# One queue for the bulk loads, and block 1's convolution inputs turned by TensorE

## The chip, the cores and the metric

The kernel runs on one NeuronCore of a Trainium2 chip. A core has a matrix engine (TensorE, called PE in the profile; its weight loads are the row PEld), a vector engine (VectorE, DVE), a scalar engine (ScalarE, ACT), a general engine (GpSimd, POOL) and a sync engine (SyncE, SP), which here only issues transfers. All read and write one on-chip memory, SBUF, of 128 partitions; PE writes to a second one, PSUM. Transfers (DMAs) are issued by SP, ACT or POOL and carried by 16 DMA engines. SP's transfers run on one queue (q1 in the profile), ACT's on q10, POOL's on q0. The metric is the device time of one execution in microseconds (us); lower is better.

## The reference

The inputs are bfloat16: q, k, v of 2048 x 640, filters `ssm_k` of 640 x 2048, four taps per channel (`shift_k`), a vector `ssm_D`, and the three weight matrices of a gated feed-forward layer (640 x 1728 twice, 1728 x 640).

```
k_shift[s] = sum over t of k[s + t - 3] * shift_k[:, 3 - t]     # a causal convolution with 4 taps
kv         = k_shift * v
y          = irfft(rfft(kv, padded) * rfft(ssm_k, padded))[:S]   # a causal convolution as long as the sequence
y          = y + kv * ssm_D
h          = q + layernorm(q) * y
h2         = h + (silu(LN(h) @ w_gate) * (LN(h) @ w_up)) @ w_down
```

## The kernel before

The sequence is cut into four blocks of 512 rows (`block_j`, j = 0 to 3), the 640 channels into two halves of 320 (`c`). A block's rows are laid out four to a partition, b = 0 to 3.

The long convolution is done by a transform written as matmuls. `fwd` (L585) does the first stage: a matmul per b with a constant table, a copy from PSUM to SBUF, and four transfers ("shuffles", named `sh`) that regroup partitions. It is called for the filter (K) and for kv (X) of each block and half. `spec` (L609) is the second stage, 16 or 32 small 32 x 32 matmuls per step; `swap` (`sw`) exchanges real and imaginary rows by two transfers; `product` multiplies spectra on DVE; `inv2` goes back, and four transfers named `rs` regroup again. `conv_bp` ends the convolution, multiplies by the layer norm of q and adds q. All these shuffles are SBUF-to-SBUF transfers issued by SP. For block j the products use this block's and earlier blocks' spectra, so block j needs the filter's and kv's block j.

What feeds this stage, k, v and the filters, is prepared in two ways:

- Block 0 (`kv_first`, L550): k is loaded as plain rows (`KN0`), turned by PE (`kr`, into `KTR`), and the four taps are matmuls with diagonal matrices (`DIAG`, built by `diag`) that add up in PSUM (`kvp`, 24 matmuls for each b); DVE multiplies by v (`kvv`). The filter is loaded by ACT's queue (`kraw00`, `kraw01`) and turned by PE (`k_natural`, L521).
- Blocks 1 to 3 (`load_kv`, L484, and `kv_block`, L734): k is loaded with its three preceding rows (`kin`), and v (`vin`), both on POOL's queue; DVE multiplies by the taps and adds (4 multiplies, 3 adds, 1 product with v for each half, on 128 x 1280 elements). For blocks 2 and 3 the adds are accumulating transfers on POOL (`KACC`). The filter (`load_kraw`, L498, where `KDMA` is true) is loaded by a transposing transfer (`kraw`), stored to DRAM (`kst`) and loaded again (`kld`) to get four rows to a partition, all on SP.

After the convolution of a block, `ln_bp` normalizes h, PE turns it (`tr`) and a copy puts it into `HNT` (`te`). `ffn_pair` computes the gate and up products of two groups of 128 columns (`gu`), `ffn_b` the down-projection (`dn`), the final add (`fa`) and the store (`st`). The weights are loaded once, by `load_weights` (L894), in 18 pieces on POOL's queue; each piece waits for the piece before the last, and the first two for a product of block 0's kv. q of block 0 (`x0`) is loaded by SP, of the later blocks by POOL (`load_x`).

Nothing is ordered at run time. Every operation is given a number when the program is built, and `_PLAN` (L1058 on) lists all operations in one order with the engine that does each one; this gives each engine its own fixed list. An entry such as `46,4,0,594` is operation 46, on engine 4 (0 PE, 1 ACT, 2 DVE, 3 POOL, 4 SP), then two planned numbers, of which only the order and the choice of buffers and semaphores follow, and for some a letter for the PSUM pool. An engine goes through its list in order and waits, where a buffer or an input needs it, on semaphores (`Prog.emit`, L130). So an operation that waits holds up everything behind it on its engine, and on SP it holds up the issue of all later transfers.

Helpers carry most of the lines that the profile shows: L425 issues every plain transfer, L434 is nearly every matmul, L416/L417 and L419/L420 are copies out of PSUM, L637 is every two-operand DVE operation, L504 a transposing transfer, L535 and L561 are the transposes of block 0's filter and k.

Of the kernel before, what the change touches and what calls it, by code (L numbers as in the profile page):

```python
# [279 lines left out]
def bass_sequential_preLN__ssm_conv_h3__swiglu_ffn__prompt_kernel(  # L280
# [6 lines left out]
    R = 4  # L287
# [6 lines left out]
    KDMA = [False, True, True, True]  # L294
# [13 lines left out]
    with ExitStack() as es:  # L308
# [71 lines left out]
        WROW = P.tile("wrow", None, P.poolbases["TMP"][0])  # L380
        P.pool("KRAW", slots(1, 4 * CW), True)
        P.pool("KT", slots(1, 4 * CW), True)
        P.pool("TB", slots(2, 8 * CW), True)
        P.pool("UK", slots(10, 2 * CW), True)
# [3 lines left out]
        P.pool("SK", slots(4, 8 * CW), True)  # L388
        P.pool("E", slots(4, 4 * CW), True)
# [33 lines left out]
        def dma(subs, kb, reads, writes, prio, eng="sp", after=(), name="", kind="load"):  # L423
            kw = dict(accum_op=ALU.add) if kind == "acc" else {}
            fns = [(lambda g, d=d, s=s: g.dma_start(d(), s(), **kw)) for d, s in subs]  # L425
            return P.op({eng: (0.9 if eng == "pool" else 0.5) * len(subs)}, fns, reads, writes, prio, after=after, dma=(kb, kind), name=name)
# [23 lines left out]
        dma([(lambda: V(WROW, 0, 4 * D, 0, 1), lambda: dram(A_shift_k, 0, [[4 * D, 1], [1, 4 * D]]))], 5, [], [(WROW, 0)], 40, name="taps")  # L450
# [17 lines left out]
        def taps_natural(prio):  # L468
            for k in range(4):
# [13 lines left out]

        def load_kv(j, c, prio):  # L484
# [4 lines left out]
            def rows(p0, p1):  # L489
# [4 lines left out]
            dma(subs, 560, [], [(kt, 0)], prio, name=f"kin{j}{c}", eng="pool", after=turned[:1])  # L494
            dma([(lambda: V2(vt, 0, CW, 4, CW), lambda: dram(V2d, B * j * D + c * CW, [[R * D, 128], [D, 4], [1, CW]]))],
                328, [], [(vt, b) for b in range(4)], prio + 1, name=f"vin{j}{c}", eng="pool", after=turned[:1])

        def load_kraw(j, c, prio):  # L498
            if KDMA[j]:
# [6 lines left out]
                    [], [(t, 0)], prio, after=turned[:1], dma=(328, "turn"), name=f"kraw{j}{c}")  # L506
# [9 lines left out]
        def load_x(j, prio):  # L516
            t = xts[j] = P.tile(f"x{j}", "XH")
            dma([(lambda: V(t, 0, 4 * D), lambda: dram(X2, B * j * D, [[R * D, 128], [1, R * D]]))], 655, [],
                [(t, (b, c)) for b in range(4) for c in range(2)], prio, name=f"x{j}", eng="pool" if j else "sp", after=[kv_last[0, 0]] if j == 1 else ())
# [28 lines left out]
        turned = []  # L548

        def kv_first(prio):  # L550
            dma([(lambda: V(KN0, 0, 4 * D), lambda: dram(K2, 0, [[R * D, 128], [1, R * D]]))], 655, [], [(KN0, 0)], 10, name="kn0")
            for c in range(2):
                dma([(lambda c=c: V2(VIN0, c * 4 * CW, CW, 4, CW), lambda c=c: dram(V2d, c * CW, [[R * D, 128], [D, 4], [1, CW]]))],
                    328, [], [(VIN0, (c, b)) for b in range(4)], 12, name="vin0")
            for h in range(2):
                def turn(h):
                    pt = P.tile("pkr", "pC")
                    fns = []
                    for k in range(2):
                        for d in range(5):  # L560
                            fns.append(lambda t, k=k, d=d: t.transpose(B16(pt, k, d * 128, 128), V(KN0, (2 * h + k) * D + d * 128, 128), V(IDN, 0, 128)))  # L561
                    cells = [(KTR, 2 * h + k) for k in range(2)]
                    turned.append(pe(fns, 128, 10, [(KN0, 0), (IDN, 0)], [(pt, 0)], prio, reserve=cells, name=f"kr{h}"))
                    src = lambda: psb[:, 2 * pt.base:2 * pt.base + 2048].rearrange("p (k d e) -> p k d e", k=2, e=128)[:, :, 0:5, :]
                    evac(lambda: V3(KTR, h * 260 + 2, 130, 2, 520, 5, 128), src, 1280, [(pt, 0)], cells, prio, fast=True, name=f"kre{h}")
                turn(h)
            for b in (3, 0, 1, 2):
                def out(b):
                    pt = P.tile("pkv", "pC")
                    fns = []  # L570
                    for c, d, o, n in ((0, 0, 0, 128), (0, 1, 128, 128), (0, 2, 256, 64), (1, 2, 0, 64), (1, 3, 64, 128), (1, 4, 192, 128)):
                        for t_ in range(4):
# [3 lines left out]
                                          lambda d=d, bb=bb, sh=sh: V(KTR, d * 520 + bb * 130 + sh, 128),  # L576
                                          lambda w0=w0, n=n: V(DIAG, w0, n), t_ == 0, t_ == 3))
                    pe(fns, 128, 24, [(KTR, i) for i in range(4)] + [(KTR, "z")] + [(DIAG, d) for d in range(5)], [(pt, 0)], prio,
                       reserve=[(VIN0, (c, b)) for c in range(2)], name=f"kvp{b}")
                    vv = lambda: V2(VIN0, b * CW, 4 * CW, 2, CW)  # L580
                    kv_last[0, b] = vec(dve1(640), tt(vv, lambda: B32x2(pt, CW), vv, ALU.mult),
# [602 lines left out]
```

## Time and profile before

| what | us |
|---|---|
| time, median of 3 runs | 344.53 (343.39 to 345.29) |
| profiled execution: time | 347.39 |
| profiled execution: span, first to last instruction | 345.5 |
| PE busy | 276.2 (80% of the span) |
| DVE busy | 204.2 (59%) |
| ACT busy | 174.2 (50%) |
| POOL busy | 47.7 (14%) |
| chain that ended last: PE 48%, DMA 26%, ACT 9%, DVE 9%, issue 4%, SP's queue 3% | |

The profile is of one execution. Its page gives for each engine the busy time, and, in 40 equal slices of the span, tenths of busy time (9 is 90% or more); `PEclk` is the clock that was granted to PE, in tenths of the full one; `DMA` the mean busy share of the 16 DMA engines and `GB/s` what they moved. The chain of waits is followed back from the last instruction, at each step to what released it. Other answers of the trace used below are the instructions in order of time, and the busy time of each engine in stretches that are named by their start and end in us. There the columns are the length, then PE, PEld, DVE, ACT, POOL (busy us and number of instructions), the granted clock, the DMA share and GB/s. Shares over 1 come from packets that overlap.

### The profile page before, as it was taken

Reading aid. Unit: us, or ns where it says so; the run is one execution under the profiler, and the core shown is the slowest. Engines: PE = TensorE matmul, PEld = TensorE weight load, DVE = VectorE, ACT = ScalarE, POOL = GpSimd, SP = SyncE. Lnnn points to the kernel's source line nnn. Section 1 sums busy time; section 2 is a strip of 40 time slices with the busy share of each in tenths; the row PEclk is TensorE's granted clock in tenths of the full one; section 3 lists DMA queues with packets and bytes.
Section 4 is the critical chain, followed back from the end, with each engine's and each line's share of the span. In section 5 each row is a group of like instructions: output and inputs, shape, how many; then the busy total and the mean of one; then the engine's idle time right before and its main releaser. Section 6 shows DMA issues by size and latency. Waiting matters only on the chain.

```text
span 345.5 us, 8043 instructions
## 1 busy us (share of the span) xinstructions
PE 276.2 (80%) x3366; PEld 144.6 (42%) x3392; DVE 204.2 (59%) x356; ACT 174.2 (50%) x260; POOL 47.7 (14%) x64
## 2 busy tenths in 40 slices
PE   0986535424869989999799999366989999999996
PEld 0741111111424435754244556123444457544474
DVE  3586757655736848783278767738678682212502
ACT  1657967424853854527777625269736332132100
POOL 0231214302220013221121000102100020000000
PEclk9995555655899999999999999856799999999999
DMA  7869999999889749448464324662351200100001
GB/s 222 251 201 348 303 392 308 331 119 346 220 230 256 185 96 284 138 117 238 134 191 110 135 84 174 181 222 77 115 193 58 98 2 21 57 0 2 0 19 59
DMA packets 41352, 56.27 MB, mean 163 GB/s; under 512 B 12562, under 2 KB 31795, under 8 KB 41316
## 3 DMA queue, kind: packets, MB, share of 16 engines
q1 hardware_dynamic: 34788, 37.11, 33.4%
q0 software_dynamic: 5024, 17.94, 20.4%
q10 hardware_dynamic: 1504, 0.69, 0.7%
q8 instruction: 27, 0.44, 0.5%
q14 instruction: 9, 0.07, 0.1%
HBM read 19.03 MB, written 4.59 MB: 68 GB/s over the span
## 4 chain that ended last, share of the span: by engine, by line
PE 48%; DMA 26%; ACT 9%; DVE 9%; issue 4%; SPq 3%; ACTq 0%; DVEq 0%; POOLq 0%
PE ps L434 46%; DMA sb<-sb 21%; ACT sb L416 7%; DVE sb L637 7%; SPq L425 3%; DMA sb<-in_A_ssm_k_dram 2%; DMA out_dram<-sb 1%; ACT sb L419 1%; DMA sb<-in_A_q_dram 1%; ACT sb L721 1%; DVE stt L683 1%; DVE sb L417 1%; PE ps L887 1%; PE ps L535 1%; ACT sb L928 0%
## 5 line engine op out<-in xcount | busy, mean ns | idle before, releaser
L434 PE MATMUL ps<-sb 128*128 128x512 bf16 (+4 forms) x1066 | 192.4, 334 | 5.8 <-ACT sb L928 2.6
L637 DVE TENSOR_TENSOR sb<-sb 128x1280 bf16<-128x1280 bf16 (+3 forms) x152 | 110.1, 762 | 50.8 <-DMA sb<-sb 21.8
L434 PEld LDWEIGHTS ps<-sb 128*128 128x128 bf16 x1092 | 98.9, 98 | 85.7 <-issue 6.3
L434 PE MATMUL ps<-sb,tab 32*32 32x320 bf16 (+1 forms) x2176 | 81.8, 348 | 51.4 <-DMA sb<-sb 25.4
L416 ACT ACTIVATE sb<-ps 128x640 bf16<-128x640 f32 (+1 forms) x129 | 88.8, 747 | 62.8 <-PE ps L434 47.0
L434 PEld LDWEIGHTS ps<-sb,tab 32*32 32x32 f16 (+1 forms) x2176 | 35.6, 92 | 99.8 <-issue 39.9
L637 DVE TENSOR_TENSOR sb<-ps,sb 128x640 bf16<-128x640 f32 (+3 forms) x50 | 42.1, 846 | 58.7 <-PE ps L434 57.2
L928 ACT ACTIVATE sb<-ps 128x1024 bf16<-128x1024 f32 (+2 forms) x32 | 29.3, 916 | 42.3 <-PE ps L434 42.0
L942 ACT ACTIVATE sb<-ps 128x1024 bf16<-128x1024 f32 x18 | 18.5, 1025 | 21.8 <-PE ps L434 15.5
L419 ACT ACTIVATE sb<-ps 128x640 bf16<-128x640 f32 x31 | 20.3, 706 | 17.5 <-PE ps L434 17.4
L708 POOL TENSOR_TENSOR stt<-stt 128x2 f32<-128x2 f32 (+1 forms) x12 | 12.4, 1034 | 72.4 <-DVE stt L706 72.4
L695 DVE TENSOR_SCALAR sb<-sb,stt 128x320 bf16<-128x320 bf16 (+1 forms) x48 | 16.8, 391 | 5.3 <-PE ps L887 3.1
L425 POOL DMA_DIRECT2D sb<-sb x12 | 10.9, 909 | 51.6 <-DVE sb L637 45.9
L683 DVE BATCH_NORM_STATS2 stt<-sb 128x6 f32<-128x320 bf16 x40 | 17.6, 478 | 0.1
L417 DVE CAST sb<-ps 128x640 bf16<-128x640 f32 x12 | 9.8, 822 | 10.3 <-PE ps L434 10.3
L535 PE MATMUL ps<-sb 128*128 128x128 bf16 (+1 forms) x24 | 3.7, 254 | 8.6 <-DMA sb<-in_A_ssm_k_dram 8.6
L721 ACT ACTIVATE sb<-sb 128x640 bf16<-128x640 bf16 x12 | 8.8, 733 | 3.2 <-DMA sb<-in_A_q_dram 3.1
L729 ACT ACTIVATE sb<-sb,stt 128x640 bf16<-128x640 bf16 x12 | 10.0, 836 | 0.2
L425 POOL DMA_DIRECT2D sb<-in_A_v_dram x6 | 4.7, 788 | 35.6 <-PE ps L434 35.6
L425 POOL DMA_DIRECT2D sb<-in_A_k_dram x6 | 6.0, 1000 | 25.1 <-DVE sb L637 13.9
L809 DVE SCALAR_TENSOR_TENSOR sb<-ps,sb 128x640 bf16<-128x640 f32 x8 | 6.4, 817 | 2.9 <-PE ps L434 2.9
L887 PE MATMUL ps<-sb 128*128 128x128 bf16 x80 | 7.2, 250 | 0.2
(27 smaller groups left out, 46.6 us busy)
## 6 DMA issues: line engine op xcount, KB each, us to landing
sb<-sb SPq DMA_DIRECT2D x160, 160.0 KB, 3.9
sb<-sb POOLq DMA_DIRECT2D x12, 320.0 KB, 4.5
sb<-in_A_k_dram POOLq DMA_DIRECT2D x6, 560.0 KB, 6.2
out_dram<-sb SPq DMA_DIRECT2D x16, 160.0 KB, 2.2
sb<-in_B_w_gate_dram POOLq DMA_DIRECT2D x5, 416.0 KB, 6.2
sb<-in_B_w_up_dram POOLq DMA_DIRECT2D x5, 416.0 KB, 6.6
sb<-in_A_v_dram POOLq DMA_DIRECT2D x6, 320.0 KB, 4.9
k_nat<-sb SPq DMA_DIRECT2D x6, 320.0 KB, 5.9
```

Source lines behind the costliest of these rows:

```text
L416: fns = {"act": lambda a: a.activation(out=dst(), in_=src(), func=ACTF.Copy), "dve": lambda v: v.tensor_copy(out=dst(), in_=src())}
L417: "dve": lambda v: v.tensor_copy(out=dst(), in_=src())}
L419: fns = {"act": lambda a: a.activation(out=dst(), in_=src(), func=ACTF.Copy, scale=scale), "dve": lambda v: v.tensor_scalar(out=dst(), in0 ...
L425: fns = [(lambda g, d=d, s=s: g.dma_start(d(), s(), **kw)) for d, s in subs]
L434: return lambda t: t.matmul(o(), l(), r(), start=st, stop=sp)
L637: return lambda v: v.tensor_tensor(out=o(), in0=a(), in1=b_(), op=op)
L683: vec(dve1(CW, False), lambda v: v.bn_stats(st6(l, j, b, c), V(xt, b * D + c * CW, CW)), [(xt, (b, c))], [(ST, ("s", j, b, c))], prio, nam ...
L695: vec(dve4(n), lambda v: v.tensor_scalar(out=dst(), in0=src(), scalar1=m, scalar2=rs(l, j, b), op0=op, op1=ALU.mult), reads + [(ST, cell), ...
L708: P.op({"pool": 1.05}, lambda g: g.tensor_tensor(out=y, in0=va, in1=stt[:, 420:420 + hi - lo], op=ALU.pow), c1 + [(ST, "half")], c3, prio, ...
L721: P.op({"act": act_c(D) + 0.05}, lambda a, b=b, jk=jk: a.activation(out=V(jk, 0, D), in_=V(xt, b * D, D), func=ACTF.Copy, accum_out=tmv(l, ...
L928: P.op({"act": act_c(n)}, lambda a: a.activation(out=dst(), in_=src(), func=ACTF.Silu), rd, wr, -1000, name=f"si{j}{i}")
L942: P.op({"act": act_c(1024)}, lambda a: a.activation(out=V(ub, 0, 1024), in_=B32x2(u, 512), func=ACTF.Copy), [(u, 0), (u, 1)], [(ub, 0)], - ...
```

## The change

Bulk loads move to SP's queue. `load_kv`, `load_x` and `load_weights` lose their `eng="pool"`, and with it the waits that spread the loads in time (`turned`, `kv_last`, the chain of weight pieces). Two waits are new: block 2's first k and v loads wait for the last readers (`users`) of buffers that now hold block 1's data.

Block 1 is prepared as block 0 is. `kv_first` becomes `kv_pe(j)` and is called for j = 0 and j = 1: k as rows, 20 transposes on PE, 96 diagonal matmuls, 4 products on DVE, and for j = 1 a small copy (`hal`) that takes the last rows of block 0's turned k as the halo. v is loaded in one transfer per block. The filter of block 1 is loaded for both halves in one transfer (`krf1`) and turned by 20 transposes on PE (`k_one`). Block 1's transposing loads, stores and second loads, its `kin` and `vin` and its `kv_block` are gone. `fwd` gets a `step` for the new layout.

The taps' row buffer moves, the cost of an SP issue in the planner goes from 0.5 to 0.62, and `_PLAN` is new (1129 operations for 1136). On SP's list 227 issues stand for 202 (195 operations for 170; 32 of them, the swaps, issue two), on POOL's 12 for 45. The new SP list begins: tab0, drow, kn0, x0, krf1, vf0, x1, vf1, wg1, wu0, wg3, taps, wu2, wu4, tab1, kn1, the four shuffles shK00, wu1, wg2, three of shX00, wg4, the fourth, gul, swW000, wg0, three of shK01, swW001, the fourth, wu3, rs00h1, swW010, rs00h0, the four shX01, rs00h2, rs00h3, two of shK10, a piece of wd, swW011, another of wd, two of shK10, swW100, the four rs01, and then the four shX10. The transposing loads of blocks 2 and 3 stand so: kraw20 after rs10h0 and before shX11G0, kraw21 after kld20 and before rs11h3, kraw30 after kst21 and before shK20G0, kraw31 between shuffles of shX21. Before, kraw20 stood after kld11 and before swW011, and kraw21 between the last rs01 and shK11G0. On PE's list, 6 steps stand between block 1's last down-projection and block 2's first gate group, where 21 stood.

```diff
-    KDMA = [False, True, True, True]
+    KDMA = [False, False, True, True]
...
+        KN = [KN0, P.tile("kn1", None)]
+        KTRS = [KTR, P.tile("ktr1", None, P.poolbases["KIN"][0] + 8 * CW)]
+        VF = [VIN0, P.tile("vf1", None, P.poolbases["KIN"][0])]
+        KRF = P.tile("krf", None)
+        KT1 = P.tile("kt1", None, P.poolbases["KRAW"][0])
+        WROW = KN0
...
+        def users(*ts):
+            return [o for o in P.ops if any(t in ts for t, _ in o.reads)]
...
-            dma(subs, 560, [], [(kt, 0)], prio, name=f"kin{j}{c}", eng="pool", after=turned[:1])
+            late = users(KTRS[1], VF[1]) if (j, c) == (2, 0) else ()
+            dma(subs, 560, [], [(kt, 0)], prio, name=f"kin{j}{c}", after=late)
...
-                [(t, (b, c)) for b in range(4) for c in range(2)], prio, name=f"x{j}", eng="pool" if j else "sp", after=[kv_last[0, 0]] if j == 1 else ())
+                [(t, (b, c)) for b in range(4) for c in range(2)], prio, name=f"x{j}")
...
-        def kv_first(prio):
-            dma([(lambda: V(KN0, 0, 4 * D), lambda: dram(K2, 0, [[R * D, 128], [1, R * D]]))], 655, [], [(KN0, 0)], 10, name="kn0")
...
+        def kv_pe(j, prio):
+            kn, ktr, vf = KN[j], KTRS[j], VF[j]
+            dma([(lambda: V(kn, 0, 4 * D), lambda: dram(K2, B * j * D, [[R * D, 128], [1, R * D]]))], 655, [], [(kn, 0)], 10 if j == 0 else 30, name=f"kn{j}")
+            dma([(lambda: V(vf, 0, 4 * D), lambda: dram(V2d, B * j * D, [[R * D, 128], [1, R * D]]))],
+                655, [], [(vf, b) for b in range(4)], 12 if j == 0 else 31, name=f"vf{j}")
+            if j:
+                halo.append(vec(0.2, lambda v: v.tensor_copy(out=V3(ktr, 1, 520, 5, 130, 4, 1), in_=V3(KTRS[0], 129, 520, 5, 130, 4, 1)),
+                                [(KTRS[0], i) for i in range(4)], [(ktr, "z")], prio, name="hal"))
...
+        def k_one(prio):
+
+            dma([(lambda: V2(KRF, 0, B, 5, B), lambda: dram(A_ssm_k, B, [[S, 128], [128 * S, 5], [1, B]]))], 655, [], [(KRF, 0)], 29, name="krf1")
+            old = users(kts[0, 0])
+            for h in range(2):
+                def turn(h):
+                    pt = P.tile("pKT", "pC")
+                    fns = []
+                    for k in range(2):
+                        for d in range(5):
+                            def f(t, k=k, d=d):
+                                a = sb[:, KRF.base + d * B + 2 * h + k:KRF.base + d * B + 2 * h + k + 1]
+                                src = bass.AP(a.tensor, a.offset, [list(a.ap[0]), [R, 128]])
+                                return t.transpose(B16(pt, k, d * 128, 128), src, V(IDN, 0, 128))
+                            fns.append(f)
...
+            if j == 1:
+                UKt[j, c] = fwd(f"K{j}{c}", KT1, lambda b: b, c * CW, "UK", pb + 99, D)
...
+            if j > 1:
                 kv_block(j, c, pb + 100)
...
             def piece(subs, kb, cells, nm):
-                chain.append(dma(subs, kb, [], cells, 35, eng="pool", after=(chain[-2:-1] or [kv_last[0, 0]]) + (front if nm[:2] == "wd" else []), name=nm))
+                dma(subs, kb, [], cells, 35, after=front if nm[:2] == "wd" else [], name=nm)
...
-            for c in range(2):
+            for c in range(2 if j != 1 else 0):
...
             if j == 0:
+                k_one(300)
+                kv_pe(1, 301)
                 taps_natural(500)
```

## The prediction

> **What bounds the kernel now.** I read the page's slices first. TensorE (PE) is busy 80% of the span, but not evenly: from about 26 us to 105 us its digits fall to 2-6, the granted clock is 0.5 for most of that stretch, and the DMA row stands at 9. After that PE is nearly full, with one dip near 60% of the span, where the clock falls again.
>
> ```profile
> PE   0986535424869989999799999366989999999996
> ...
> PEclk9995555655899999999999999856799999999999
> DMA  7869999999889749448464324662351200100001
> ```
>
> Then the chain of waits in order of time, for the first 100 us. Its long pieces are SBUF-to-SBUF transfers (columns: start, length, what): the regrouping of each conv step, called shuffles here.
>
> ```profile
> 20.37 2.22 DMA sb<-sb
> ...
> 26.78 5.19 DMA sb<-sb
> ...
> 37.85 8.06 DMA sb<-sb
> ...
> 53.80 5.64 DMA sb<-sb
> ...
> 61.12 7.59 DMA sb<-sb
> ...
> 70.54 10.35 DMA sb<-sb
> ...
> 82.86 4.62 DMA sb<-sb
> ...
> 98.34 3.52 DMA sb<-sb
> ```
>
> These are all 160 KB or pairs of it. In a quieter queue the same step takes 3.52 us at 98.34 and 3.89 us at 125.66, so I call 3.7 us its uncrowded price. What crowds it is seen in the timeline and in busy time by stretch (PE, weight loads, DVE, ACT, POOL, clock, DMA share, GB/s):
>
> ```profile
> 64.15 6.28 SPq L504 DMA_TRANSPOSE sb<-in_A_ssm_k_dram  x1
> ```
>
> ```profile
> 2.40:12.40 10.00, 3.78 (x29) 2.79 (x30) 4.65 (x9) 1.75 (x2) 0.19 (x1) 1.00 0.97 293
> 72.00:74.00 2.00, 1.04 (x5) 0.60 (x6) 0.28 (x1) 0.00 (x0) 0.00 (x0) 0.50 1.37 53
> 80.00:84.00 4.00, 2.33 (x52) 0.69 (x52) 0.33 (x1) 1.78 (x4) 1.87 (x3) 0.50 1.04 390
> 213.50:229.00 15.50, 7.47 (x170) 3.54 (x169) 9.83 (x13) 6.75 (x11) 1.35 (x2) 0.75 0.71 220
> 229.00:246.00 17.00, 13.41 (x223) 6.98 (x224) 12.80 (x29) 14.75 (x29) 2.05 (x2) 0.62 0.33 121
> ```
>
> Behind the transposing load of block 2 (kraw21) the DMA engines are fully busy and move 53 GB/s; a few us later they move 390. While PE waits for this, block 0's gate and up groups cannot start: the last copy before them (te01, on DVE at 89.69 for 0.82 us) ends at 90.5. From there to the end PE works 227.7 of 255 us, so PE bounds the rest, except in the dip at 213.5-246.
>
> **The change, part by part.** Sums are made against the profiled execution (span 345.5, its time 347.39, 2.86 us above the median of the runs, 344.53) and then taken off the median.
>
> *Block 1's filters and k.* Gone from SP's queue ahead of block 0's last shuffles are two transposing loads, two stores to DRAM and two loads back; kraw20 and kraw21 are also moved behind them, past rs01 (block 0's last regrouping). Three chain steps hold a transposing load: 37.85 (kraw11, issued at 33.43), 61.12 and 70.54 (kraw21). Their excess over 3.7 us is 4.36 + 3.89 + 6.65 = 14.9 us, and I take it all off. The other crowded steps (26.78, 53.80, 82.86) have 1.49 + 1.94 + 0.92 = 4.35 us more, which plain loads cause; those loads stay, so this stays. Bounds of the gain: 0, if the loads now in the same queue crowd just as much, and 19.25.
>
> [...] The row above shows 53 GB/s with all engines busy. [...]
>
> *What replaces them on PE.* 40 transposes of 128x128 (10 took 0.56 us and 20 took 2.32 us in the timeline, so 56 to 116 ns each: 2.2 to 4.6 us) and 96 diagonal matmuls. The same matmuls of block 0 took 4.58 us for 79, 58 ns each: 5.6 us, or 11.1 at half clock. PE is busy 22.9 of the 40 us from 20 to 60, so the 17.1 idle us cover them in amount. But PE runs in order, and the four groups of 24 stand between block 0's conv steps; one that comes just before a step that is ready delays it by 24 x 58 ns = 1.4 us, 2.8 at half clock. I take one such delay, +3 us; bounds 0 and 11.1. On DVE, 16 tensor operations of 820 ns (13.1 us) go; four multiplies from PSUM of 820 ns, four copies of 1280 columns (823 ns, or 1247 on ACT) and a small halo copy come. DVE is busy 27.8 of those 40 us and waits on shuffles, so I price this at nothing: the crowded shuffles hide it, bounds -2 and 0.
>
> *Bulk loads to SP's queue.* 29 loads leave POOL. SP's issues go from 202 to 227, POOL's from 45 to 12 (the accumulating ones). The price is what stands in front. Ahead of the first shuffle (shK00) SP's queue now holds 6.95 MB (K: tables 384 KB, seven loads of 640 KB, five weight pieces of 416 KB), and ACT's 0.68 MB of idents and block 0's filters: 7.81 million bytes in all. At 340 GB/s (midway between 293 and 390 above) from the first packet at 2.4 us that is 25.4 us; the first shuffles landed at 20.37 + 2.22 = 22.59. So +2.8 us, bounds -0.2 (390) and +6.5 (293). Between there and rs01 stand eight more weight pieces, 3.03 million bytes, 7.8 us of queue time at 390; before, POOL's copies of such loads filled the same stretch (337 GB/s, share 1.06 from 31.2 to 60), so their cost is the 4.35 us that I left in. SP's own 25 extra issues of about 0.6 us stand mostly in the front, behind the queue's data, and cost nothing while the queue is full; once it is empty each delays a shuffle by 0.6 us.
>
> [...]
>
> *Waits added.* kin20 (block 2's k) waits on SP for the last readers of block 1's k and v tiles, and behind it stand swW110, vin20, block 1's regrouping and kraw20. Those readers are PE's steps of block 1, column half 1, and whoever waits behind them needs these first, so I price it at nothing; should they be late, each us is a us for i2 of block 1, which FFN groups of block 0 then cover.
>
> *Moved transposing loads.* kraw20 and kraw21 now fall in the stretch where PE has block 0's groups. Two others fell there before (kraw30 at 94.80, kraw31 at 111.28), and the chain steps that followed were 106.93: 5.54 and 118.20: 4.29 us, 1.8 and 0.6 above 3.7, so 1.2 each: +2.4 us, bounds 0 and 2 x 6.65.
>
> *The order.* In the old table 21 conv steps with no group between them stand on PE's list after block 1's last down-projection, and only then block 2's first gate group. That is the dip: 32.5 us (213.5 to 246) in which PE did 7.47 x 0.75 + 13.41 x 0.62 = 13.9 us of full-clock work, 18.6 lost. In the new table six steps stand there, and 17 conv steps instead of 11 lie between the down-projections. The fill is taken from work that was due later, so the end moves by what is filled. I take half, -9.3 us, because the shuffles between those steps still have their latency; bounds -18.6 and -2. What is late next is block 3's conv, then PE itself. The hole at 160-172 (2.59 us idle, waiting for x2 behind a store) keeps its cause: 0, bounds -2.6 and 0.
>
> Sum: -14.9 + 2.8 + 3 + 2.4 - 9.3 = -16.0 us. 347.39 becomes 331.4 for a profiled execution, and 344.53 becomes **328.5**.
>
> **The rivals.**
> *More of it.* All 19.25 us of crowding go, PE's groups hide, and 15 of the 18.6 us are filled: -19.25 + 2.8 + 2.4 - 15 = -29, 315.5. For it: PE's 17 idle us. Against it: the front still moves as many bytes.
> *One of the two gains fails.* Without the dip's gain beyond 2 us: -16 + 7.3 = -8.7, 335.8; without the transposing loads' gain but for a third: -16 + 9.9, 338.4. Against: both mechanisms have their own rows.
> *No change.* Crowding stays as it was (0 for 14.9): -1.1, 343.4. This is the case where the loads are hidden or harmful just as before, whichever queue has them.
> *Slower: shuffles held behind loads in one queue.* Place: SP's queue from the first shuffle to rs01. If it moves only 243 GB/s, as the first 10 us of the trace did, the first shuffles land at 34.5 (+11.9) and the 3.03 MB add 12.5 us, all on the chain: 11.9 + 12.5 - 14.9 + 3 + 2.4 - 9.3 = +5.6, 350.1. It decides from 280 GB/s downward (10.84 MB / r = 39.0 us), with all of the weights on the chain. For it: nothing ever queued so much ahead of a shuffle. Against it: 390 to 407 GB/s wherever no transposing load is in the queue.
>
> **How the numbers follow.** A measurement of this kernel can tell about 0.5% (1.7 us) from no change. Chances: the forecast, taken as 320 to 335, 0.42; more of it 0.20; one gain failing (335 to 342.8) 0.20; no change 0.04; slower 0.14. So faster 0.82, same 0.04, slower 0.14. The best ends of the terms together give about 306, the worst about 370. The range leaves some 0.06 below 309 and 0.13 above 346. The likeliest case's own range is 320 to 335.
>
> **What would show it.** Right: no chain step over 6 us before te01; te01's end between 76 and 86 us instead of 90.5; first shuffles landing near 25; the stretch from 20 to 60 with PE above 30 us busy; no stretch of 15 us after 107 with PE under 60% busy. Wrong: shuffles that take 8 us and more behind 400-GB/s loads; PE waiting on DMA in the middle of block 0's groups behind kraw20 or kraw21; the dip back at a clock of 0.6.

## The result and the profile after

| | before | after |
|---|---|---|
| time, median (lowest to highest), 4 runs each | 344.46 (343.39 to 345.29) | 316.23 (312.92 to 316.78) |
| profiled execution: time / span | 347.39 / 345.5 | 316.17 / 314.4 |
| te01 (last copy before block 0's groups) ends | 90.5 | 73.5 |
| from there to the end of the span | 255.0 | 240.8 |

The ratio is 0.9162 [0.9094, 0.923]: 28.2 us less, where 16.0 were forecast. The time lies in the range (309 to 346), but below the likeliest case's own 320 to 335; it is the size of the rival "more of it" (315.5). Both halves of the sum were too small. Up to te01 17.0 us went (9.1 forecast), behind it 14.1 (6.9 forecast); a second profile of the changed kernel, shown below, has 17.8 and 8.9. Some executions of one kernel take 1.5% and more longer than its fastest; the ratios given here leave them out, but the profiled executions of after_again, before_plain_all, after_pool_loads and after_pool_spaced are among them.

The slices of the changed kernel, TensorE's busy tenths, its clock and the DMA share:

```profile
PE   1999768778896989897899998998999999999995
...
PEclk9997996558999999999999999999999999999999
DMA  7997967759999699769695056634243110100011
```

In the old kernel the clock was near half in seven slices on end (26 to 86 us) and again in the dip. Here three slices, 47 to 71 us, are at 5 or 6, the dip is gone, and the DMA row, at 9 for most of the old front, drops to 5 to 7 there, but for one slice, once the loads at the start are through. The chain of waits of the changed kernel, its transfer steps up to block 0's groups and a little beyond (start, length, what):

```profile
3.63 7.93 DMA sb<-in_A_ssm_k_dram
...
35.30 4.66 DMA sb<-sb
...
45.59 2.12 DMA sb<-sb
...
53.26 3.89 DMA sb<-sb
...
57.90 2.73 DMA sb<-sb
...
78.02 5.17 DMA sb<-sb
```

No shuffle on the chain before te01 takes over 5 us, where the old kernel had 8.06, 7.59 and 10.35. The busy time by stretch of the changed kernel (length; PE, PEld, DVE, ACT, POOL with instructions; clock, DMA share, GB/s) for the places that the prediction spoke of:

```profile
2.40:12.40 10.00, 5.20 (x37) 3.48 (x37) 6.34 (x14) 4.46 (x4) 0.00 (x0) 1.00 1.03 325
12.00:20.00 8.00, 8.00 (x87) 6.64 (x87) 5.95 (x20) 5.97 (x11) 1.02 (x1) 1.00 1.02 409
2.40:22.00 19.60, 14.80 (x150) 11.51 (x150) 13.62 (x35) 11.40 (x17) 1.02 (x1) 1.00 1.03 364
34.00:41.00 7.00, 5.10 (x143) 3.06 (x140) 5.89 (x9) 6.11 (x10) 1.65 (x1) 1.00 0.92 284
41.00:48.00 7.00, 4.61 (x114) 2.94 (x110) 3.89 (x6) 5.14 (x9) 0.00 (x0) 1.00 0.62 229
64.00:74.00 10.00, 7.90 (x173) 4.33 (x175) 8.88 (x23) 8.96 (x15) 2.02 (x2) 0.56 0.54 167
184.00:209.00 25.00, 22.31 (x371) 14.57 (x385) 20.73 (x39) 12.39 (x19) 1.53 (x2) 1.00 0.61 213
```

And the same three stretches of block 0's convolution in the old kernel:

```profile
34.00:41.00 7.00, 3.72 (x87) 1.39 (x86) 5.81 (x8) 6.15 (x11) 2.02 (x3) 0.50 1.05 274
41.00:48.00 7.00, 2.44 (x22) 0.54 (x20) 3.15 (x6) 5.51 (x12) 1.10 (x2) 0.50 1.02 385
64.00:74.00 10.00, 2.10 (x53) 0.84 (x38) 3.92 (x6) 3.39 (x6) 2.25 (x3) 0.67 1.14 250
```

The reader is to see three things. The bulk loads at the start run at 409 GB/s from one queue between 12 and 20 us; the front as a whole, from 2.4 to 22 us, moves 364 GB/s (7.14 MB), where the forecast took 340. While block 0 convolves, the DMA engines are now 54 to 92% busy, where they had been at 102 to 114%. And between block 1's down-projections and block 2's first groups (184 to 209 us) PE is busy 22.31 of 25 us at full clock and loses 2.7 us, where the dip had lost 18.6.

### The profile page after: what moved, and what is told of

Same layout as the page of the kernel before. It is cut to its first block, busy times and chain, and to the rows that moved or that the text cites. A ratio compares the mean times of both kernels' runs of the same rounds, so it can differ in the third digit from the quotient of the medians.

```text
span 314.4 us, 8325 instructions
## 1 busy us (share of the span) xinstructions
PE 275.2 (88%) x3502; PEld 151.9 (48%) x3528; DVE 211.0 (67%) x366; ACT 164.2 (52%) x243; POOL 23.1 (7%) x31
## 4 chain that ended last, share of the span: by engine, by line
PE 36%; DMA 30%; DVE 18%; issue 6%; ACT 4%; SPq 3%; ACTq 1%; POOL 0%; DVEq 0%; POOLq 0%
PE ps L441 34%; DMA sb<-sb 25%; DVE sb L671 12%; SPq L432 3%; DMA sb<-in_A_ssm_k_dram 3%; DVE stt L717 2%; DVE sb L424 2%; ACT sb L423 2%; DMA sb<-in_A_q_dram 2%; DMA out_dram<-sb 1%; PE ps L922 1%; ACTq L432 1%; ACT sb L755 1%; DVE sb L729 1%; DVE sb L841 1%
## 5 line engine op out<-in xcount | busy, mean ns | idle before, releaser
L441 PE MATMUL ps<-sb 128*128 128x512 bf16 (+3 forms) x1162 | 197.9, 325 | 9.9 <-ACT sb L976 3.0
L441 PEld LDWEIGHTS ps<-sb 128*128 128x128 bf16 x1188 | 104.7, 100 | 89.0 <-issue 5.2
L671 DVE TENSOR_TENSOR sb<-sb 128x1280 bf16<-128x1280 bf16 (+3 forms) x136 | 97.8, 755 | 30.2 <-DMA sb<-sb 16.5
L423 ACT ACTIVATE sb<-ps 128x640 bf16<-128x640 f32 (+1 forms) x114 | 78.7, 743 | 51.0 <-PE ps L441 34.4
L441 PE MATMUL ps<-sb,tab 32*32 32x320 bf16 (+1 forms) x2176 | 72.8, 323 | 17.5 <-DVE sb L671 5.5
L671 DVE TENSOR_TENSOR sb<-ps,sb 128x640 bf16<-128x640 f32 (+3 forms) x54 | 45.5, 846 | 42.6 <-PE ps L441 42.0
L424 DVE CAST sb<-ps 128x640 bf16<-128x640 f32 x26 | 21.0, 820 | 10.8 <-PE ps L441 10.7
L426 ACT ACTIVATE sb<-ps 128x640 bf16<-128x640 f32 x29 | 19.0, 700 | 13.9 <-PE ps L441 13.7
L432 POOL DMA_DIRECT2D sb<-sb x12 | 10.8, 901 | 80.7 <-DVE sb L671 76.1
L573 PE MATMUL ps<-sb 128*128 128x128 bf16 x40 | 3.6, 266 | 6.8 <-DMA sb<-in_A_k_dram 6.8
L424 DVE COPY sb<-ps 128x1280 bf16<-128x1280 bf16 x8 | 6.5, 822 | 3.0 <-PE ps L922 1.3
L922 PE MATMUL ps<-sb 128*128 128x128 bf16 x80 | 6.8, 243 | 0.9 <-DVE sb L729 0.7
L465 DVE TENSOR_TENSOR sb<-sb 128x512 bf16<-128x512 bf16 x5 | 3.2, 689 | 5.9 <-DMA sb<-in_A_shift_k_dram 5.9
```

Source lines behind the costliest of these rows:

```text
L423: fns = {"act": lambda a: a.activation(out=dst(), in_=src(), func=ACTF.Copy), "dve": lambda v: v.tensor_copy(out=dst(), in_=src())}
L424: "dve": lambda v: v.tensor_copy(out=dst(), in_=src())}
L426: fns = {"act": lambda a: a.activation(out=dst(), in_=src(), func=ACTF.Copy, scale=scale), "dve": lambda v: v.tensor_scalar(out=dst(), in0 ...
L441: return lambda t: t.matmul(o(), l(), r(), start=st, stop=sp)
L671: return lambda v: v.tensor_tensor(out=o(), in0=a(), in1=b_(), op=op)
```

## The experiments

Two theories stood at the start. **T**, the forecast's: transposing loads clog the engines (14.9 us), the queue as such costs a little (+2.8), and the order fills half of the dip. **Q**: it is the queue; loads and shuffles no longer run beside each other, whatever the loads' kind. The old kernel, run again beside the experiments, had medians of 346.22 to 348.26 us where it had 344.46 in the result, and the changed kernel itself, run again beside the last three experiments, had this expectation and result:

> The changed kernel as it is, beside the three below on the same chip. 314 to 319, ratio 0.91 to 0.92; it gives the value that the next runs are held against.

319.21 us (314.28 to 321.09), ratio 0.9224 [0.9007, 0.9442]; te01 at 72.7. So a difference of 3 us between medians of runs made at different times says nothing, and the ends of te01 (72.7 and 73.5 in two executions of the same kernel) tell more. Behind te01 those two executions differ by 5.2 us. Where a part of the span is compared below, it is this:

| kernel | time | span | te01 ends | te01 to end |
|---|---|---|---|---|
| before | 344.46 | 345.5 | 90.5 | 255.0 |
| before_plain_block2 | 342.04 | 340.4 | 84.7 | 255.7 |
| before_plain_all | 340.36 | 341.6 | 86.3 | 255.3 |
| before_plain_late_wd | 344.27 | 342.3 | 82.5 | 259.8 |
| after | 316.23 | 314.4 | 73.5 | 240.8 |
| after_again | 319.21 | 318.7 | 72.7 | 246.0 |
| after_two_turns | 322.88 | 319.6 | 75.9 | 243.7 |
| after_pool_loads | 335.8 | 335.3 | 84.1 | 251.2 |
| after_pool_spaced | 341.17 | 342.3 | 88.4 | 253.9 |
| after_weights_spread | 324.28 | 321.8 | 79.0 | 242.8 |
| after_one_tap | 320.07 | 318.1 | 73.4 | 244.7 |
| after_downs_in_a_row | 332.04 | 329.0 | 73.0 | 256.0 |
| after_filters_on_sp | 316.46 | 313.8 | 73.0 | 240.8 |

### What the transposing loads cost

The old kernel with the transposing loads of block 2, or all six, replaced by plain loads of the same bytes:

```diff
-                P.op({"sp": 1.5}, [lambda g: g.dma_start_transpose(
-                    out=V2(t, 0, CW, 4, CW), in_=dram(A_ssm_k, c * CW * S + B * j, [[S, CW], [1, B]]))],
+                P.op({"sp": 1.5}, [lambda g: g.dma_start(
+                    V(t, 0, 4 * CW), dram(A_ssm_k, c * CW * S + B * j, [[S, 128], [1, 4 * CW]]))],
```

> The kernel before, with block 2's two transposing loads (kraw20, kraw21) made plain loads of the same bytes into the same buffers at the same places. Block 2's filter is then not turned and its values are others; every other instruction keeps its shape. Theory T (the transposing loads crowd the shuffles of block 0): the chain steps at 61.12 and 70.54, 7.59 and 10.35 us, fall to 4 to 5 us, te01 ends near 80 instead of 90.5, and the time is 8 to 11 us under the 344.5 of before. Theory Q (the plain loads on POOL's queue crowd them): the steps stay over 6 us, and the time is within 3 us of before.

> The kernel before, with all six transposing loads made plain loads of the same bytes (the filters of blocks 1 to 3 are then not turned; values are others, shapes the same). T: the 14.9 us of the prediction's first term and a few us more behind kraw30 and kraw31, 13 to 18 us under before, te01 near 75 to 77. Q: within 4 us of before.

Measured: 342.04 us, ratio 0.9812 [0.9718, 0.9907], and 340.36, ratio 0.9704 [0.9594, 0.9814]. Both gain, and both less than T said; against the 344.5 of before the medians are 2.4 and 4.1 us lower, about what Q said. In the profiles te01 came 5.8 and 4.3 us earlier, and h011, the residual add behind block 0's last regrouping, did not come earlier at all (76.35 and 77.62, against 76.51). Here is why, first the chain of before_plain_block2, then its busy time by stretch:

```profile
41.24 8.03 DMA sb<-sb
...
57.87 10.97 DMA k_nat<-sb
...
71.21 4.96 DMA sb<-sb
```

```profile
57.00:64.00 7.00, 4.38 (x74) 1.33 (x72) 6.17 (x11) 6.24 (x11) 3.25 (x4) 0.50 0.89 244
64.00:74.00 10.00, 1.70 (x21) 0.92 (x22) 2.39 (x3) 1.90 (x3) 2.23 (x3) 0.50 1.04 392
```

No transposing load runs there any more, the engines move 392 GB/s from 64 to 74 us, and PE still does 1.70 us of work in 10. The step up to h011 is as long as before, filled now by other loads (kin20 and the down-projection's weights from POOL) and by the store of the filter, which takes 10.97 us and for which SP's next load waits. There the transposing load had been the visible occupant of a step that was crowded anyway. It was not so behind h011: the step that took 10.35 us from 70.54 in the old kernel, while kraw21 was landing, takes 4.96 here. These 5.4 us are most of the 5.8 gained at te01, and for this one step the 6.65 of the forecast was nearly right.

The other way round, two transposing loads were added to the changed kernel, at the places of the old kraw11 and kraw21:

```diff
+        def extra(n):
+            P.op({"sp": 1.5}, [lambda g: g.dma_start_transpose(
+                out=V2(DUM[n], 0, CW, 4, CW), in_=dram(A_ssm_k, n * CW * S + 2 * B, [[S, CW], [1, B]]))],
...
+    for n, after in enumerate(("shK01G3", "rs01h2")):
+        k = next(k for k, x in enumerate(out) if names[x[0]] == after)
+        out.insert(k + 1, (d0 + n, 4, out[k][2], out[k][2] + 6.0, []))
```

> The changed kernel with two transposing loads added that nothing needs, into free space, at the old places of kraw11 (behind the last shK01) and of kraw21 (behind the last rs01). T: the two steps behind them grow by 4.4 and 6.7 us as before, 324 to 329. Q (a transposing load hurts only together with POOL's loads): under 3 us more than 316.2.

322.88 us (321.4 to 326.97), ratio 0.9296 [0.9204, 0.9389], between the two expectations. The stretch up to te01 grew by 2.3 us (3.2 against after_again), traceable at its place: shX01 lands 1.0 late behind the first; h011, whose regrouping is issued ahead of the second, is 2.2 late, so the second adds next to nothing before te01. In the busy time by stretch the first one is plain to see; the same stretch of the changed kernel stands second:

```profile
36.00:44.00 8.00, 5.70 (x156) 3.71 (x140) 5.63 (x10) 6.49 (x10) 1.65 (x1) 1.00 0.99 216
```

```profile
36.00:44.00 8.00, 6.08 (x162) 4.04 (x161) 6.29 (x10) 6.76 (x11) 1.65 (x1) 1.00 0.78 259
```

The DMA share goes from 0.78 to 0.99 while the rate falls from 259 to 216 GB/s: the loads do clog, as T said, but two of them cost 2.3 us and not the 11.0 (4.36 + 6.65) booked for those two places. Further down 2.8 us more come, which is within what two executions of the unchanged kernel differ by (240.8 and 246.0).

### What the queue is worth

The changed kernel with its bulk loads back on POOL's queue, once as they stand in the new order and once with the old spacing (the early ones held until block 0's products are made, each weight piece behind the piece before the last; `gate` is the product kvv00):

```diff
+    bulk = ("kin", "vin", "x1", "x2", "x3", "wg", "wu", "gul", "wd")
+    out = [(i, 3 if P.ops[i].dma and P.ops[i].name.startswith(bulk) else e, s, f, ps) for i, e, s, f, ps in out]
```

> The changed kernel, with the loads that before stood on POOL's queue (kin, vin, x1 to x3, all weights) put back on POOL, at their places in the new order and without the old spacing waits; block 1 stays prepared on PE. T: 313 to 320, as the changed kernel (316.2). Q: 8 to 17 us more, 324 to 333, with chain steps over 6 us before te01.

```diff
+    for i, *_ in early:
+        P.ops[i].deps[P.ops[gate]] = 2
+    pieces = [x[0] for x in out if x[0] in pool and names[x[0]][0] in "wg"]
+    for old, i in zip(pieces, pieces[2:]):
+        P.ops[i].deps[P.ops[old]] = 2
```

> The changed kernel with its bulk loads (kin, vin, x1 to x3 and the weights) on POOL's queue again, in the changed order, and with the old kernel's spacing: those that stood ahead of block 0's products start only behind the second of them, and each weight piece waits for the piece before the last. The changed kernel is at 316.2 us; with the same loads on POOL without spacing it was at 335.8, where block 0's filter (ACT's queue) landed 7 us late. Theory Q (two queues that share the engines crowd each other all through block 0 and 1, so one queue in order is itself the gain): spacing brings back only the front, about 7 us of the 14 to 19; 325 to 332. Rival F (the unspaced flood at the start did it all): 315 to 320. Theory T as forecast (the queue alone is worth -2.8 the other way): 311 to 316.

335.8 us, ratio 0.9582 [0.9469, 0.9695], and 341.17 us (336.93 to 344.1), the latter outside all three ranges expected of it. Moving the same loads to the other queue costs 20 us by the medians and 12 to 15 by the ratios (0.9582 against 0.9224 and 0.9162), and spacing does not bring it back. But the two runs do not price the queue cleanly, since each brings a wait of its own. Chain of after_pool_loads:

```profile
3.59 15.90 DMA sb<-in_A_ssm_k_dram
```

Block 0's filter, loaded on ACT's queue, takes 15.90 us instead of 7.93 beside a queue that POOL fills at once, and the kernel starts 7.5 us late (kvv02, the last of block 0's products, at 30.4 for 22.9). Chain of after_pool_spaced:

```profile
22.39 4.45 DMA sb<-in_A_q_dram
```

Here x1, held back, arrives at 26.8, while ACT's list in the new order has its layer norm early: ACT waits, and kvv02 ends at 34.3. From kvv02 to te01 the two take 53.7 and 54.1 us, where the changed kernel takes 50.7; so it is the front in the main, and 3 us between. Behind te01 they lose 10.3 and 13.1 us more against the first profile of the changed kernel (5.1 and 7.8 against the second). There POOL's list is in order too, and its loads (kin21, the down-projection's weights) stand behind accumulating transfers that wait for DVE (in the changed kernel's trace POOL idles 80.7 us before its 12 such transfers, and DVE ends 76.1 us of it). My +2.8 for the queue would make the move a gain, and it cost 12 to 20 us. But the move also changes when the loads start and what they wait for, and how much of the 12 to 20 us is the sharing of the engines and how much the lists' order these two don't tell.

Two runs ask the old kernel instead. The five pieces of the down-projection's weights, four of which POOL issues at 60 to 69 us beside the last regrouping, are put behind vin20 at 82 us:

```diff
+    m = [x for x in out if names[x[0]] == "wd"]
+    out = [x for x in out if x not in m]
+    k = next(k for k, x in enumerate(out) if names[x[0]] == "vin20")
+    at = out[k][3]
+    out[k + 1:k + 1] = [(i, e, at, at + f - s, ps) for i, e, s, f, ps in m]
```

> The old kernel with the five pieces of the down-projection's weights (2.4 MB, four of them issued between 60 and 69 us, while the last regrouping of block 0, rs01, is under way) put behind vin20 on POOL's list, at 82 us. Theory P (POOL's loads share the 16 engines with the shuffles and make them slow; my forecast left 4.35 us of this in place and gave all of 14.9 us to the transposing loads): h011, the residual add behind rs01, ends 2 to 5 us earlier than 76.5, te01 2 to 4 us earlier than 90.5, 340.5 to 342.5 us. Theory T (the transposing load kraw21 at 64 to 70 us holds this step, whatever POOL loads): te01 within 1 us of 90.5 and 343.5 to 345.5.

> The same late weights, and besides all six transposing filter loads made plain row loads (so the filters of blocks 1 to 3 are not turned, and the output is wrong there). With plain loads alone te01 ended at 86.3 and h011 at 77.6, no earlier than in the old kernel. Theory P: with both causes gone h011 ends at 69 to 73 and te01 at 76 to 81, nearly the 73.6 of the changed kernel; ratio 0.945 to 0.96. Theory T: te01 stays at 84 to 87, ratio 0.965 to 0.975, and the rest of the changed kernel's lead in block 0 has another cause.

With the transposing loads in place: 348.28 us (343.13 to 361.83), ratio 1.0057 [0.9979, 1.0136], no gain. Its profiled execution had a span of 360.0 us, far from most of its times, so its steps are not compared. With plain loads: 344.27, ratio 1.0024 [0.9961, 1.0088]. Its busy time by stretch, beside those of before_plain_all, which come second:

```profile
64.00:74.00 10.00, 4.12 (x58) 1.53 (x58) 5.08 (x8) 2.99 (x5) 0.00 (x0) 0.50 0.88 304
82.00:92.00 10.00, 8.58 (x189) 4.17 (x190) 4.93 (x10) 8.10 (x11) 2.79 (x4) 1.00 0.94 317
```

```profile
64.00:74.00 10.00, 0.50 (x16) 0.18 (x16) 3.35 (x5) 2.58 (x5) 2.11 (x4) 0.50 1.03 373
82.00:92.00 10.00, 8.68 (x196) 5.08 (x197) 8.71 (x17) 8.05 (x11) 2.22 (x3) 0.83 0.81 233
```

With four of the five pieces out of the step, PE does 4.12 us of work there and not 0.50; h011 ends at 73.9 for 77.6, te01 at 82.5 for 86.3. Against before_plain_block2, whose kraw11 still transposes, it is 2.5 us at h011 and 2.2 at te01. That is the crowding by plain loads, shown at its place: 2.2 to 3.7 us, where the forecast had put all of it at 4.35. But the bytes come down later on block 1's shuffles (the DMA share from 82 to 92 goes from 0.81 to 0.94, DVE's busy time from 8.71 to 4.93), and from te01 to the end 4.4 us are lost again. Theory P's number for te01 (76 to 81) was missed by 1.5 us, and its time by far; Theory T's time was missed too. This kernel has the six plain loads that gave a ratio of 0.9704 above, and is not faster than before; whether the late weights cost those 3% or the 3% was partly chance is not shown.

Where do the bytes cost nothing, then? The changed kernel loads 2.13 MB of weights ahead of the first shuffles. These five pieces were put behind the last shX00, in one burst (`first` is the place of shK00G0):

```diff
+    first = next(k for k, x in enumerate(out) if names[x[0]] == "shK00G0")
+    moved = [x for x in out[:first] if names[x[0]][:2] in ("wg", "wu")]
+    out = [x for x in out if x not in moved]
+    k = next(k for k, x in enumerate(out) if names[x[0]] == "shX00G3")
+    at = out[k][2]
+    out[k + 1:k + 1] = [(i, e, at, at + f - s, ps) for i, e, s, f, ps in moved]
```

> The changed kernel with the five weight pieces that stand ahead of the first shuffles on SP's queue (2.13 MB) put one by one behind later shuffles (shX00G3, shK01G3, rs00h0, rs00h3, shK10G3). My term of +2.8 us for the loads in front of the first shuffles says: 5.2 to 6.3 us of queue time less ahead, so the first shuffles land up to 3 us earlier and the time is 311 to 314.5. Rival: the queue is nearly empty when the first shuffles are issued (the front moved 404 to 415 GB/s, not 340), and the front's 3 to 4 us come from ACT's filter load and PE's order: first shuffles unchanged within 1 us, and the pieces now crowd later shuffles: 316 to 321.

324.28 us (322.99 to 327.38), 5.1 above after_again's median. Other than the expectation says, the kernel that ran does not spread the pieces: SP issues all five between 31.8 and 34.4 us. The first shuffles went out as before (shK00's last issue ends at 23.9 us; 24.6 and 23.7 in two executions of the changed kernel) and the last of them landed about 1 us earlier (25.4; 26.5 and 26.3), so little had waited behind those weights. The shuffles behind the burst paid. Chain and busy time of after_weights_spread:

```profile
35.53 6.78 DMA sb<-sb
```

```profile
34.00:41.00 7.00, 2.58 (x46) 1.69 (x46) 1.46 (x2) 3.12 (x5) 0.00 (x0) 0.95 1.00 329
41.00:48.00 7.00, 3.66 (x71) 2.22 (x72) 4.75 (x7) 2.60 (x4) 1.65 (x1) 0.50 0.79 301
```

The chain's step at 35 us (swW000, the first transfer behind the burst) is 6.78 long, where the longest shuffle on the changed kernel's chain before te01 took 4.66; the DMA share is 1.00 instead of 0.92, PE's work half, and te01 comes 5.4 us later. This prices one place against another: ahead of the first shuffles these bytes cost PE nothing that these runs show, in one burst behind them 5 us. What they would cost one by one behind later shuffles is not shown.

### Whether the front can still be had

The front itself is 2 to 4 us later in the changed kernel (the last copy of the filter's first stage, e1K00b3, ends at 20.6 for 17.8), and its chain begins with the filter on ACT's queue, whose last part lands at 11.56. The 8.57 in the old kernel's chain is the half that was issued first there; its other half landed at 11.77, so the whole filter is not later now. The two loads of this filter were put on SP's queue, behind kn0:

```diff
+    m = [x for x in out if names[x[0]] in ("kraw00", "kraw01")]
+    out = [x for x in out if x not in m]
+    k = next(k for k, x in enumerate(out) if names[x[0]] == "kn0")
+    at = out[k][3]
+    out[k + 1:k + 1] = [(i, 4, at, at + f - s, ps) for i, e, s, f, ps in m]
```

> The changed kernel with block 0's two filter loads taken from ACT's queue and put on SP's, right behind kn0. In the changed kernel this filter lands at 11.6 us instead of 8.6, beside 3.9 MB that SP issues from 1.6 to 5.7 us, and the chain of waits begins with it. Theory (a load that is needed first has to stand first in the one queue, since two queues share the engines): the filter lands at 6 to 8 us, its last turn's copy (kte00) ends at 11 to 13 instead of 15.0, te01 1.5 to 3.5 us earlier, 312.5 to 315 if the changed kernel is at 316.2. Rival: PE then waits for k, x0 and v, which come as much later, and the first shuffles meet a queue that is still full: within 1.5 us of the changed kernel or slower.

316.46 us (315.48 to 321.07), ratio 0.9229 [0.9112, 0.9345]. kte00 ended at 13.9, 1.0 earlier, e1K00b3 at 20.3 and te01 at 73.0: the changed kernel's values. The last part of the filter landed at 8.5 us, and the rival held: PE, busy 8.00 of the 8 us from 12 to 20 in the changed kernel and 7.43 here, sets the pace there, not the filter's transfer. On PE's new list 48 diagonal matmuls of block 0 (13.65 to 18.1 us) stand ahead of the filter's first stage, which the old list had ahead of them.

### Block 1's work on TensorE

```diff
-                        for t_ in range(4):
+                        for t_ in (range(4) if j == 0 else (3,)):
...
-                                          lambda w0=w0, n=n: V(DIAG, w0, n), t_ == 0, t_ == 3))
+                                          lambda w0=w0, n=n: V(DIAG, w0, n), t_ == 0 or j == 1, t_ == 3))
```

> The changed kernel, where block 1's k takes one of its four taps: 24 diagonal matmuls instead of 96, so 72 x 58 ns = 4.2 us of PE work less (8.4 at half clock). Leaves out three taps of the short convolution of block 1. My term was +3 us for block 1's work on PE, of which this takes three quarters of the matmuls: 313 to 315, with te01 1.5 to 3 us earlier. Rival A (PE's idle time covers them wholly): within 1 us of 316.2 and te01 unchanged. Rival B (they all lie on PE's path, which is 80% busy from 20 to 60 us): 308 to 312.

320.07 us (315.24 to 322.21) with te01 at 73.4: 72 matmuls less, and nothing gained, as rival A said. Its busy time by stretch shows more than that:

```profile
34.00:41.00 7.00, 5.67 (x85) 2.46 (x86) 5.83 (x10) 5.75 (x10) 1.65 (x1) 0.50 0.89 286
41.00:48.00 7.00, 5.06 (x84) 2.29 (x82) 4.26 (x6) 5.82 (x10) 0.00 (x0) 0.74 0.66 243
```

With all four taps the clock is 1.00 in both stretches (shown above, and again in after_again), with one tap 0.50 and 0.74, and PE is busy a little longer for the smaller work. The matmuls stand in holes of PE's list, and where they stand the clock of the whole stretch, the convolution steps between them included, is 1.00. That they pay for themselves by this is a reading of one profile; that PE's idle time would hide them at either clock is not excluded.

### The dip

Block 1's four down-projections one behind the other, ahead of the convolution steps that the new order put between them:

```diff
+    for what, after in ((('dn100', 'dn105', 'dn1010', 'fa10', 'st10'), 'st13'), (('dn110', 'dn115', 'dn1110', 'fa11', 'st11'), 'st10'), (('dn120', 'dn125', 'dn1210', 'fa12', 'st12'), 'st11')):
+        m = [x for x in out if names[x[0]] in what]
+        out = [x for x in out if x not in m]
+        k = next(k for k, x in enumerate(out) if names[x[0]] == after)
+        at = out[k][2]
+        out[k + 1:k + 1] = [(i, e, at, at + f - s, ps) for i, e, s, f, ps in m]
```

> The changed kernel with block 1's four down-projections one behind the other on PE's list, where the new order has conv steps between them; some 19 conv steps then stand without a group between them before block 2's first gate group, as 21 did in the old order. Theory T (that cover is what filled the dip, which I priced at 9.3 of 18.6 us lost): 325 to 333, with a new stretch behind the down-projections in which PE is under 65% busy. The stretch from 184 to 209 us now loses 2.7 us. Rival: the conv steps there wait for DVE and transfers in any order, and PE has the same total work: within 3 us of 316.2.

332.04 us (329.68 to 336.67): 12.8 above the changed kernel's median beside it, and 15.2 in the span from te01 to the end against the first profile (10.0 against after_again's). Its busy time by stretch:

```profile
184.00:198.00 14.00, 14.00 (x203) 9.50 (x197) 6.01 (x9) 4.92 (x7) 0.00 (x0) 1.00 0.34 118
198.00:225.00 27.00, 17.00 (x239) 9.17 (x252) 16.54 (x32) 10.50 (x16) 1.53 (x2) 0.65 0.47 158
```

First PE is full, then it idles and its clock falls: 27 us (198 to 225) in which it did 17.00 x 0.65 = 11.05 us of full-clock work, 15.9 lost. The old dip is back, with the same operations on every engine. This shows the mechanism, and with the 2.7 us lost in the changed kernel that nearly all of the 18.6 us could be filled.

## Why the prediction was right and wrong

*The sum.* -16.0 forecast, -28.2 measured; in the profiled spans -31.1, of which 17.0 up to te01 and 14.1 behind. The direction, the two places and the bound behind te01 (PE) were right. "More of it" was the case that came, with other shares than it assumed; that its 315.5 is so near 316.23 is luck.

*Transposing loads, -14.9.* The step that failed: I gave a crowded shuffle's whole excess over 3.7 us to the transposing load that ran in it. Made plain, that held for one step of the three. The one at 70.54 fell from 10.35 to 4.96 us. The one at 61.12 still led to h011 at 76.3 and 77.6 us for 76.5, and behind the one at 37.85 the last shX01 landed, with all six plain, at 52.7 us for 52.4. At te01 block 2's two loads were worth 5.8 us and all six 4.3, by the ratios 1.9 and 3.0% (6.5 and 10 us); two put back cost 2.3 us at te01. The row (53 GB/s at full DMA share) was right about the load and wrong as a price for every step, for other loads take up the room at 373 to 392 GB/s. The measured gain lies between none and the forecast's 14.9.

*Plain loads, 4.35 left in.* Too small, and counted as staying. Taking four weight pieces from beside the last regrouping is worth 2.2 to 3.7 us at te01, in a step whose excess I had given to a transposing load; and in the changed kernel no shuffle on the chain before te01 is over 4.66 us, so this crowding went as well. How the 17.0 us divide between the loads' kind, their queue and place, the stores and second loads of block 1's filter that are gone, DVE's lighter list and the full clock from 34 to 48 us was not told apart.

*Bulk loads in front, +2.8.* The size came near, by luck, and the cause was another. The last of the first shuffles landed at 26.5 us for 22.6, where I had 25.4. But the front ran at 364 GB/s where I took 340; when these shuffles were issued, at 22 us, 7.14 of the 7.81 MB had moved, and with 2.13 MB less ahead they landed only 1 us earlier, from which PE gained nothing. That a shuffle waits for every byte that stands ahead of it in its queue was my assumption; no run shows it by itself. The shuffles were issued 4.2 us later because of PE's fuller front. With it the rival "slower: shuffles held behind loads in one queue" fell: the front was far from the 280 GB/s at which it decides. With the loads on POOL the time was 335.8 and 341.2 us, though in an order not made for it.

*Block 1 on PE, +3.* For 72 of the 96 matmuls measured as nothing: te01 73.4 without them. The 40 transposes were not tried by themselves. I had bounded the term by 0 and 11.1 and taken one delay; I had not thought of the clock, which is higher where the extra work stands (1.00 from 34 to 48 us, with 24 of the 96 matmuls 0.50 and 0.74). Within its bounds, mis-sized.

*Moved kraw20 and kraw21, +2.4.* They stand in the groups' stretch as said (issued at 75.7 and 96.4), and the chain's steps there take 5.17 us at 78.02, 4.12 at 84.67, 7.81 at 91.24 and 5.29 at 104.58; PE is busy 14.41 of the 16.4 us behind te01. This term was not tried by itself. Its price was read from the wrong step in one case: behind kraw30 (94.80) the next step is that at 98.34, of 3.52 us, and not that at 106.93. The added wait cost nothing: kin20 is issued at 70.97, right behind swX101.

*The order, -9.3.* The mechanism was right and the half was too little: 2.7 us of loss are left in the place of 18.6, and undoing it costs 10 to 15 us. My reason for the half, that shuffles between those steps keep their latency, does not hold when each wait has a down-projection to stand behind.

*The signs named.* No shuffle over 6 us on the chain before te01 (the filter's load has 7.93, as it had 6.29), PE over 30 us busy from 20 to 60 (31.88), no 15-us stretch under 60% after 107: as said. The first shuffles landed at 26.5 for "near 25". te01 between 76 and 86: it was earlier, 73.5, which by itself showed the first half of the sum to be too small.

## What to carry to other kernels

When a transfer on the critical chain is slow, ask what else would fill the engines if the visible culprit were gone, before its whole excess is booked as a gain; in the old kernel with block 2's two or all six transposing loads made plain, the DMA share from 64 to 74 us stayed at 1.04 and 1.03, at 392 and 373 GB/s. Move bulk bytes to a time at which no short transfer is waited for, here the first 22 us, in which one queue and ACT's small one moved 364 GB/s: putting 2.13 MB of them behind the first shuffles in one burst cost 5 us, and moving others from one crowded step to a later one gained nothing. A stretch where PE waits between short steps is best filled with large groups already ready, and it may gain twice, by the work and by the clock (1.00 where the dip had 0.62 to 0.75).

## What the runs showed of the hardware that was not expected

- One queue, SP's, moved 409 GB/s from DRAM for 8 us (12 to 20 us of the changed kernel); with ACT's small loads it moved 364 GB/s from 2.4 to 22 us.
- Adding matmuls to a sparse stretch cost nothing that these runs show: the granted clock was 1.00 with 96 diagonal matmuls and 0.50 to 0.74 with 24, and te01 ended at the same time (73.5 and 73.4).
- The last part of the same two filter loads on ACT's queue (320 KB each) landed in 7.93 us beside SP's loads alone and in 15.90 us when POOL's queue was full as well.
- Taking the down-projection's weight pieces (2.13 MB) away from one step and giving them to a later one left the time of the old kernel where it was (ratio 1.0057 [0.9979, 1.0136]); with plain filter loads the step that was relieved ended 2.5 to 3.7 us earlier, and the time was still that of before (1.0024 [0.9961, 1.0088]).
